# Linear attention and a highway layer: turns of k and q in 64-row tiles, scores and state in equal row halves, gates on Pool, transfers that wait for the fifth last, and a new order

## The chip, the core and the metric

The kernel runs on one core of one Trainium2 chip. The core has a matrix engine (TensorE, PE in the profile; its weight loads are PEld), VectorE (DVE), ScalarE (ACT), GpSimd (POOL) and SyncE (SP, which here only issues transfers), and 16 DMA engines that move data between device memory (DRAM) and the on-chip memory SBUF. TensorE writes its results into PSUM, eight banks of 2 KB per partition, from which DVE or ACT copy them; POOL doesn't read PSUM here. Each engine takes its own instructions in order, and semaphores hold it back where it needs another's result. The metric is device microseconds of the program, as the median of several runs.

## The reference

There are 4 batches, 8 heads, 768 positions and 64 channels. The first part is attention with a decay `lam` per head, in blocks along the sequence with a state of 64 x 64 per head:

```
intra = (qb @ kb^T) * Dmask          # Dmask[i, j] = lam^(i-j) for j <= i
out   = intra @ vb + (qb * lam^(pos+1)) @ kv_state
kv_state = lam^block * kv_state + (kb * lam^(block-1-pos))^T @ vb
```

The second part is a highway layer over the 3072 rows of 512 that come out of it:

```
H = max(x @ w_h, 0);  T = sigmoid(x @ w_t + b_t);  out = T * H + (1 - T) * x
```

All inputs and the output are float32. The inputs q, k and v are 18.9 MB together, the weights 2.1 MB, the output 6.3 MB.

## The kernel before

The work is cut into 12 steps n = 0 to 11, three for each batch, of 256 positions each and all 8 heads. Within a step the positions lie as two halves b of 128. A partition holds two neighbouring positions (j = 0, 1). The powers of `lam` are put into q and v (q times lam^t, v times lam^-t), so that the decay needs no work of its own and the mask is a plain triangle. Heads are taken in pairs hp = 0 to 3, with e = 0, 1 for the head within a pair: channels of head e lie on partitions 64e to 64e+63 of the turned k and q. The highway layer runs on the same steps (here called groups g = 0 to 10; step 11 is cut into the two groups 11 and 12 of 128 rows).

The order is written out by hand: `PLAN` is a list of tokens, and the program emits each token's instructions in that order; each engine then keeps its share of that order. A token such as `TK.3.2=3` is an operation (TK), its step (3), its part (2 means all heads; 0 and 1 are halves), and after `=` the PSUM banks that it uses. `@` names the engine. The tokens:

- `Lk`, `Lq`, `Lv` (L170): one load of 256 KB, half the heads of a step, in pieces of 512 bytes. `W` (L176): one load of 512 KB of the weights. `ST` (L337, L356): a store, 512 KB for a whole step. All of them are issued by SP, in the order of the list. `WC` casts weights to bf16.
- `CK` (L183): k to bf16. `CQ`, `CV` (L190): q and v times their powers, to bf16. Most stand on POOL.
- `TK`, `TQ` (L204): k and q are turned on TensorE against a 128 x 128 identity, 8 matmuls of 128x128 for a whole step. `EK`, `EQ`: the turned values are copied out of PSUM to SBUF, 1024 elements per partition, by ACT or DVE.
- `SS.n.e` (L224): 16 score matmuls of head parity e (on rows 64e to 64e+63 of the array), alternating one by one with the 16 matmuls (L221) that add half b = 1 - e of the step to the state (on the other 64 rows). In the third step of a batch the state after half 1 isn't needed, and `SS.n.0` has scores only. `S` and `U` are the same, apart, for step 0. `KE` copies the state out as the next half's `ss`.
- `M` (L255): a score bank times the triangle, PSUM to SBUF, on DVE. `I` (L271): turned q times the state. `A` (L281): masked scores times v, 16 matmuls of 64x64 tiles for one half of the head pairs. `D`: the result is copied to SBUF as `xT`.
- `F.g.u.w` (L300): 8 matmuls of the highway layer, half u of the output columns, w = 0 for w_h (bank `h`), 1 for w_t (bank `t`). `H` (L305): max(h, 0) - x, on DVE. `G` (L314): the sigmoid on ACT, written back to the PSUM bank. `X` (L318): gate times `hm`, on DVE, giving `th`.
- `R` (L347): x + T (H - x) is turned back to rows, 32 matmuls of 64 rows by 128 columns with 64 moving columns, as two row halves r that write two banks; `E.n.r` (L101 on ACT, L103 on DVE) copies each to the output buffer `o`, of which there are five. The last step is turned by L327 in three parts.
- `Z` (L366): matmuls on a blank tile whose result nobody reads, at the start.

SBUF buffers rotate through pools whose depths stand in `BUFS` (kf, qf and vf, the loaded tiles, have five each). A store or load on SP waits for the semaphore of the transfer eight before it, since eight semaphores are used in turn.

Of the kernel before, what the change touches and what calls it, by code (L numbers as in the profile page):

```python
# [17 lines left out]
Lk.0.0 Lv.0.1 Lv.0.0 Lq.0.0 Lk.0.1 Lq.0.1 Lv.1.1 CK.0.0@POOL Lq.1.0 Z.12=0 TK.0.0=0 Lq.1.1 CV.0.0@DVE Lk.1.0  # L18
CQ.0.0@POOL EK.0.0@DVE Lv.1.0 CV.0.1@DVE CK.0.1@ACT Lk.1.1 Z.11=1 TQ.0.0=1 B=2 EQ.0.0@ACT CQ.0.1@POOL W.0.1 W.0.0
Z.6=0 TQ.0.1=3 TK.0.1=4 EQ.0.1@DVE U.0.0 EK.0.1@ACT W.1.1 S.0.0=56 KE.0.0@DVE S.0.1=01 CQ.1.2@POOL W.1.0 M.0.0.1 Z.1=3  # L20
U.0.1 I.0=34 M.0.1.1 KE.0.1@ACT Lk.2.1 M.0.0.0 A.0.1 M.0.1.0 TQ.1.2=0 Lq.2.1 CV.1.2@DVE CK.1.2@ACT EQ.1.2@ACT Lq.2.0
Z.8=1 TK.1.2=1 A.0.0 EK.1.2@DVE Lk.2.0 D.0.0@DVE Z.3=5 SS.1.1=56 WC.0.0.1@ACT WC.0.0.0@POOL M.1.1.0 KE.1.0@ACT
WC.0.1.0@POOL D.0.1@ACT Lv.2.1 WC.0.1.1@DVE Z.4=0 SS.1.0=01 M.1.1.1 I.1=35 KE.1.1@ACT Lv.2.0 F.0.0.0=4 WC.1.1.0@DVE PT
M.1.0.1 Lk.3.1 F.0.1.0=6 M.1.0.0 WC.1.0.0@POOL WC.1.0.1@ACT Lk.3.0 WC.1.1.1@DVE A.1.1 A.1.0 BC F.0.0.1=1 H.0.1 Lq.3.1
D.1.1@ACT H.0.0 D.1.0@ACT F.0.1.1=0 Lq.3.0 CQ.2.2@POOL F.1.0.0=2 Lv.3.0 G.0.1@ACT CK.2.2@DVE F.1.0.1=6 Lv.3.1
G.0.0@ACT X.0.1@DVE TQ.2.2=5 Lq.4.0 X.0.0@DVE TK.2.2=4 EQ.2.2@ACT CV.2.2@POOL F.1.1.0=3 Lq.4.1 EK.2.2@DVE G.1.0@ACT
H.1.0 SS.2.0=01 Lk.4.1 H.1.1 CK.3.2@POOL SS.2.1=54 Lk.4.0 M.2.0.1 F.1.1.1=2 KE.2.0@ACT M.2.1.0 Lv.4.0 TK.3.2=3 M.2.1.1
CQ.3.2@POOL G.1.1@ACT I.2=15 M.2.0.0 Lv.4.1 A.2.1 X.1.0@DVE A.2.0 Lk.5.0 R.0=40 D.2.0@ACT D.2.1@DVE CV.3.2@POOL
TQ.3.2=6 E.0.0@ACT Lk.5.1 F.2.1.1=1 E.0.1@ACT EQ.3.2@DVE Lq.5.1 EK.3.2@ACT X.1.1@DVE F.2.1.0=5 CQ.4.2@POOL Lq.5.0
R.1=40 H.2.1 SS.3.1=62 Lv.5.0 F.2.0.0=3 CK.4.2@POOL KE.3.0@ACT M.3.1.1 Lv.5.1 E.1.1@ACT M.3.1.0 SS.3.0=52 E.1.0@ACT  # L30
H.2.0 Lq.6.0 TQ.4.2=0 KE.3.1@ACT CV.4.2@POOL M.3.0.1 TK.4.2=6 G.2.1@ACT Lq.6.1 F.2.0.1=4 M.3.0.0 EQ.4.2@ACT EK.4.2@DVE
Lv.6.0 I.3=32 A.3.0 CK.5.2@POOL A.3.1 Lk.6.1 SS.4.1=56 D.3.0@ACT D.3.1@DVE TK.5.2=0 KE.4.0@ACT M.4.1.1 Lk.6.0
F.3.0.0=2 G.2.0@ACT CQ.5.2@POOL EK.5.2@DVE Lv.6.1 SS.4.0=36 H.3.0 F.3.0.1=0 Lq.8.0 M.4.0.0 CV.5.2@POOL M.4.0.1
TQ.5.2=2 Lk.9.0 G.3.0@ACT F.3.1.0=3 X.2.1@DVE Lq.7.0 EQ.5.2@ACT X.2.0@DVE F.3.1.1=6 CQ.6.2@POOL M.4.1.0 Lq.7.1
KE.4.1@ACT I.4=14 H.3.1 G.3.1@ACT R.2=25 Lk.8.1 X.3.0@DVE A.4.0 E.2.1@ACT X.3.1@DVE A.4.1 Lk.7.1 SS.5.0=30 E.2.0@ACT
D.4.0@DVE CK.6.2@POOL SS.5.1=56 D.4.1@ACT Lk.7.0 TQ.6.2=2 M.5.0.0 KE.5.0@ACT CV.6.2@POOL TK.6.2=1 M.5.1.1 Lv.7.0
EQ.6.2@ACT F.4.1.0=4 M.5.0.1 Lv.7.1 EK.6.2@ACT F.4.0.0=3 H.4.1 Lk.8.0 M.5.1.0 I.5=62 SS.6.1=01 H.4.0 Lq.8.1 A.5.0
KE.6.0@ACT M.6.1.0 CQ.7.2@POOL R.3=45 Lv.9.1 A.5.1 M.6.1.1 SS.6.0=30 D.5.0@ACT Lv.8.0 F.4.0.1=1 M.6.0.0 D.5.1@ACT
M.6.0.1 Lk.9.1 TQ.7.2=6 G.4.0@ACT CK.7.2@POOL F.5.0.0=3 Lq.10.1 EQ.7.2@ACT F.4.1.1=2 H.5.0 Lk.10.1 E.3.1@ACT X.4.0@DVE
TK.7.2=0 CV.7.2@POOL G.4.1@ACT I.6=63 ST.0 KE.6.1@DVE F.5.0.1=5 X.4.1@DVE Lv.8.1 F.5.1.0=1 G.5.0@ACT CK.8.2@POOL  # L40
EK.7.2@DVE Lq.9.0 A.6.0 E.3.0@ACT H.5.1 A.6.1 SS.7.1=20 Lq.9.1 D.6.0@ACT D.6.1@DVE TK.8.2=4 M.7.1.1 F.6.1.0=1 Lv.9.0
EK.8.2@ACT X.5.0@DVE CK.9.2@POOL F.6.1.1=6 KE.7.0@DVE Lk.10.0 CQ.8.2@POOL H.6.1 R.4=30 SS.7.0=54 Lk.11.1 E.4.0@ACT
F.5.1.1=1 E.4.1@ACT M.7.0.1 G.6.1@ACT ST.4 M.7.1.0 TK.9.2=3 Lq.10.0 M.7.0.0 TQ.8.2=0 G.5.1@ACT CV.8.2@POOL F.6.0.0=4
EQ.8.2@DVE Lk.11.0 KE.7.1@ACT X.5.1@DVE I.7=25 EK.9.2@ACT Lq.11.0 A.7.0 H.6.0 A.7.1 CQ.9.2@POOL SS.8.0=01 X.6.1@DVE
D.7.1@ACT Lv.10.1 SS.8.1=34 M.8.0.1 D.7.0@ACT F.6.0.1=6 KE.8.0@DVE Lq.11.1 CK.10.2@POOL F.7.0.0=5 M.8.1.0 G.6.0@ACT
M.8.1.1 ST.3 TQ.9.2=1 CV.9.2@POOL H.7.0 F.7.1.0=2 EQ.9.2@ACT Lv.10.0 X.6.0@DVE TK.10.2=3 M.8.0.0 ST.1 I.8=45
EK.10.2@ACT CQ.10.2@POOL H.7.1 SS.9.1=61 A.8.1 KE.9.0@ACT M.9.1.0 A.8.0 R.5=02 M.9.1.1 SS.9.0=36 CK.11.2@POOL
E.5.1@DVE F.7.0.1=1 KE.9.1@ACT M.9.0.1 E.5.0@ACT F.7.1.1=2 D.8.0@DVE D.8.1@ACT ST.5 CQ.11.2@POOL M.9.0.0 G.7.0@ACT
Lv.11.1 TK.11.2=6 Lv.11.0 I.9=04 F.8.1.0=5 EK.11.2@ACT ST.2 X.7.0@DVE TQ.10.2=3 G.7.1@ACT H.8.1 CV.10.2@POOL F.8.0.0=1
EQ.10.2@ACT R.6=65 H.8.0 A.9.1 X.7.1@DVE A.9.0 SS.10.1=31 D.9.0@ACT D.9.1@DVE F.8.1.1=2 E.6.1@ACT M.10.1.1 F.9.1.0=0  # L50
E.6.0@DVE G.8.1@ACT M.10.1.0 ST.6 TQ.11.2=4 CV.11.2@POOL KE.10.0@DVE F.9.1.1=5 EQ.11.2@ACT X.8.1@DVE SS.10.0=16
G.9.1@ACT H.9.1 R.7=32 M.10.0.1 KE.10.1@ACT F.8.0.1=4 X.9.1@DVE E.7.0@ACT M.10.0.0 E.7.1@ACT I.10=06 SS.11.0=53
G.8.0@ACT ST.7 A.10.0 M.11.0.0 A.10.1 SS.11.1=21 D.10.1@ACT X.8.0@DVE F.9.0.0=5 KE.11.0@ACT M.11.1.0 D.10.0@ACT
F.9.0.1=6 M.11.0.1 M.11.1.1 F.10.1.0=4 G.9.0@ACT H.9.0 I.11=20 X.9.0@DVE A.11.0 A.11.1 R.8=31 D.11.0@ACT R.9=56
E.8.0@ACT F.10.0.0=2 E.9.0@DVE E.9.1@ACT E.8.1@ACT D.11.1@DVE ST.9 F.10.1.1=3 H.10.0 ST.8 F.10.0.1=6 H.10.1 G.10.1@ACT
F.12.1.1=5 G.10.0@ACT X.10.1@DVE F.11.1.1=1 F.11.1.0=0 G.12.1@ACT X.10.0@DVE F.11.0.1=2 G.11.1@ACT H.11.1 F.12.1.0=4
R.10=36 G.11.0@ACT H.12.1 X.11.1@DVE F.11.0.0=0 E.10.0@ACT X.12.1@DVE F.12.0.1=4 E.10.1@ACT H.11.0 F.12.0.0=1
G.12.0@ACT X.11.0@DVE ST.10 R.11.1.1=5 H.12.0 R.11.0.2=3 E.11.1.1@DVE X.12.0@DVE E.11.0.2@ACT ST.11.1.1 R.11.1.0=0
ST.11.0.2 E.11.1.0@DVE ST.11.1.0
"""  # L60

BUFS = dict(kf=5, qf=5, vf=5, kb=3, qb=2, vs=3, kT=2, qT=2, m=8, xT4=2, th4=2, xT2=3, xT1=2, th2=2, th1=2, hm2=3, hm1=2, tb2=2, tb1=2, ss=4, o=5, oh=2, oq=1)
# [3 lines left out]
def kernel(  # L66
# [11 lines left out]
    nc = tc.nc  # L78
# [67 lines left out]

    def groups(n, b):
        return ((n,), b) if n < N - 1 else ((n, b), 0)

    def new(key, shape, dtype=BF16, tag=None):  # L150
        if key not in made:
            tag = tag or key[0]
            made[key] = sb.tile(shape, dtype, tag=tag, name=tag, bufs=BUFS[tag])
        return made[key]

    def bank(key, i, shape, dtype=F32):
        if key not in made:
            made[key] = ps.tile(shape, dtype, tag=f"b{i}", name=f"b{key[0]}", bufs=1)
        return made[key]
# [8 lines left out]
    SRC = {"k": k, "q": q, "v": v}  # L168

    def load(x, n, p, eng):  # L170
        b, c = divmod(n, NST)
        hs = heads(p)
        (A if eng else nc.sync).dma_start(out=new((x + "f", n), [128, H, J * D], F32)[:, hs],  # L173
                          in_=SRC[x][b, hs, c * 2 * C:(c + 1) * 2 * C, :].rearrange("h (p j) d -> p h (j d)", j=J))

    def load_w(w, g):  # L176
        nc.sync.dma_start(out=w_f[w][:, 2 * g:2 * g + 2],
                          in_=(moe_w_h, moe_w_t)[w][256 * g:256 * g + 256].rearrange("(kc p) m -> p kc m", p=128))

    def cast_w(w, g, i, eng):  # L180
        copy(eng, w_b[w][:, 2 * g + i], w_f[w][:, 2 * g + i])
# [17 lines left out]
    def trans(x, n, p, bk):  # L199
        hs = heads(p)  # L200
        t = bank((x + "tr", n, p), bk[0], [128, (hs.stop - hs.start) // 2, J, C], BF16)
        for i, h in enumerate(range(hs.start, hs.stop, 2)):
            for j in range(J):
                T.transpose(t[:, i, j, :], get(x + "b", n)[:, j, h:h + 2, :], id128)  # L204

    def evac_k(n, p, eng):
        hs = heads(p)
        copy(eng, new(("kT", n), [128, NP, J, C])[:, hs.start // 2:hs.stop // 2], get("ktr", n, p))

    def evac_q(n, p, eng):  # L210
        hs = heads(p)
        copy(eng, new(("qT", n), [128, NP, J, C])[:, hs.start // 2:hs.stop // 2], get("qtr", n, p))


    def score(n, e, hp, j, b):
        T.matmul(get("s", n, e, hp // 2)[half(b), hp % 2, j, :], lhsT=get("kT", n)[half(e), hp, j, half(b)],  # L216
                 rhs=get("qT", n)[half(e), hp, :, half(b)], start=True, stop=True)
# [6 lines left out]
    def scores_state(n, e, bk):  # L224
        for u in range(2):
            bank(("s", n, e, u), bk[u], [128, 2, J, C])
        b = 1 - e
        st = [(hp, j, x) for hp in range(NP) for j in range(J) for x in range(2)]
        if b == 1 and n % NST == NST - 1:
            st = []  # L230
# [188 lines left out]
```

## Time and profile before

Four runs took 108.48, 108.48, 108.53 and 109.37 us, median 108.51. The profiled execution is the one of 109.37 us; its span, from the first to the last instruction, is 107.3 us, and 2.07 us lie around it.

| engine | busy us | share of the span |
|---|---|---|
| TensorE matmuls | 99.4 | 93% |
| TensorE weight loads | 80.6 | 75% |
| DVE | 82.4 | 77% |
| ACT | 71.8 | 67% |
| POOL | 55.6 | 52% |

From HBM 20.98 MB are read and 6.29 MB written. Matmuls are pipelined: a single one is shown with 0.19 to 0.27 us, but they start much closer together, so a group's cost on TensorE is read from the start of one group to the start of the next, or from the chain that ended last, which shows these differences. The same holds for DVE, where instructions of 512 elements last 0.68 us and start 0.60 us apart when nothing holds them. In the page's slices each digit is the busy share of one fortieth of the span (2.7 us) in tenths.

### The profile page before, as it was taken

The page shows a single profiled execution, that of the slowest core. Times are in us where ns is not written, and L with a number is a line of the kernel's source. Part 1 is how long each engine was busy: PE and PEld are TensorE (multiplying, and loading weights), DVE is VectorE, ACT ScalarE, POOL GpSimd, SP SyncE. Part 2 cuts the span into 40 slices and gives each one's busy share as a digit, 9 for nine tenths or more (in the row PEclk, how much of TensorE's full clock was granted, in tenths as well). Part 3 has the DMA queues.
Part 4 walks back from the last instruction along what each step waited for, and adds up shares of the span by engine and source line. Part 5 has one row for each costly group of instructions (what it writes and reads, how often), then busy time and mean ns, then how long its engine had stood idle before and what let it go on. Part 6 is the DMA issues. An engine that isn't in the chain of part 4 may idle for free.

```text
span 107.3 us, 4970 instructions
## 1 busy us (share of the span) xinstructions
PE 99.4 (93%) x2190; PEld 80.6 (75%) x2190; DVE 82.4 (77%) x140; ACT 71.8 (67%) x129; POOL 55.6 (52%) x46
## 2 busy tenths in 40 slices
PE   4986999999999989999999999999999999999950
PEld 1332665488987869899989888989897888889930
DVE  1233495879799786999995996999976998958860
ACT  3303244686875668689859785987696798687940
POOL 7028340427978976997548593999691700000000
PEclk9999999999999999999999999999999999999999
DMA  0899999999999999999999999999979254108264
GB/s 3 229 303 287 293 354 383 326 291 274 294 284 270 292 288 273 299 288 275 296 302 296 301 347 283 322 281 304 365 275 305 104 194 173 37 6 321 76 245 145
DMA packets 42701, 27.59 MB, mean 257 GB/s; under 512 B 1588, under 2 KB 38712, under 8 KB 42680
## 3 DMA queue, kind: packets, MB, share of 16 engines
q1 hardware_dynamic: 42528, 27.27, 86.6%
q8 instruction: 17, 0.28, 1.1%
q14 instruction: 4, 0.03, 0.1%
q10 hardware_dynamic: 152, 0.01, 0.1%
HBM read 20.98 MB, written 6.29 MB: 254 GB/s over the span
## 4 chain that ended last, share of the span: by engine, by line
PE 78%; DVE 6%; DMA 5%; issue 2%; POOL 1%; SPq 1%; ACT 1%; POOLq 0%; DVEq 0%
PE bt L300 19%; PE bh L300 18%; PE bs L216 8%; PE bo L281 6%; PE bx L347 6%; PE bqtr L204 6%; DMA qf<-in_q_dram 5%; PE bktr L204 5%; PE bspin L366 5%; PE bo L271 4%; DVE m L255 4%; PE kv L221 2%; POOL qb L190 1%; DVE hm L305 1%; SPq L173 1%
## 5 line engine op out<-in xcount | busy, mean ns | idle before, releaser
L300 PEld LDWEIGHTS <-w_b 128*128 128x128 bf16 x416 | 36.4, 98 | 4.9 <-issue 0.4
L255 DVE TENSOR_TENSOR m<-bs,tri 128x512 bf16<-128x512 f32 x48 | 31.0, 680 | 2.3 <-PE bs L216 2.1
L190 POOL TENSOR_TENSOR qb<-qf,pow_q 128x1024 bf16<-128x1024 f32 (+1 forms) x13 | 23.6, 1812 | 9.4 <-DMA qf<-in_q_dram 8.4
L314 ACT ACTIVATE bt<-bt,bt_col 128x256 f32<-128x256 f32 (+1 forms) x52 | 22.0, 432 | 5.5 <-PE bt L300 2.9
L300 PE MATMUL bh<-xT,w_b 128*128 128x256 bf16 (+1 forms) x208 | 25.0, 265 | 0.2 <-issue 0.2
L300 PE MATMUL bt<-xT,w_b 128*128 128x256 bf16 (+1 forms) x208 | 24.5, 265 | 0.0
L190 POOL TENSOR_TENSOR vs<-vf,pow_v 128x1024 bf16<-128x1024 f32 x10 | 19.0, 1904 | 7.0 <-DMA vf<-in_v_dram 6.0
L305 DVE SCALAR_TENSOR_TENSOR hm<-bh,xT 128x512 bf16<-128x512 f32 (+1 forms) x26 | 16.5, 643 | 4.0 <-PE bh L300 2.5
L318 DVE TENSOR_TENSOR th<-bt,hm 128x512 bf16<-128x512 f32 (+1 forms) x26 | 16.5, 642 | 2.0 <-ACT bt L314 1.9
L101 ACT ACTIVATE xT<-bo 128x512 bf16<-128x512 f32 x16 | 11.6, 749 | 4.6 <-PE bo L281 4.6
L216 PE MATMUL bs<-qT,kT 64*64 64x128 bf16 x384 | 13.9, 218 | 0.6 <-issue 0.3
L366 PE MATMUL bspin<-blank,id 128*128 128x512 bf16 x45 | 12.6, 425 | 1.4 <-POOL id masks.py:199 1.4
L103 POOL CAST kb<-kf 128x1024 bf16<-128x1024 f32 (+1 forms) x10 | 10.0, 995 | 6.9 <-DMA kf<-in_k_dram 5.8
L101 ACT ACTIVATE ss<-kv 128x512 bf16<-128x512 f32 x15 | 8.9, 596 | 6.4 <-PE bs L216 5.2
L216 PEld LDWEIGHTS <-kT 64*64 64x64 bf16 x384 | 10.9, 106 | 2.6 <-issue 1.1
L101 ACT ACTIVATE o<-bx 128x512 f32<-128x512 f32 x19 | 10.4, 595 | 1.4 <-PE bx L347 1.3
L101 ACT ACTIVATE qT<-bqtr 128x1024 bf16<-128x1024 bf16 (+1 forms) x10 | 9.8, 980 | 1.8 <-PE bqtr L204 1.8
L281 PE MATMUL bo<-m,vs 64*64 64x128 bf16 x384 | 9.1, 219 | 0.4 <-DVE m L255 0.4
L366 PEld LDWEIGHTS <-id 128*128 128x128 bf16 x45 | 4.4, 107 | 6.7 <-issue 2.2
L221 PE MATMUL kv<-vs,kb 64*64 64x64 bf16 x320 | 9.2, 196 | 0.0
L204 PE MATMUL bqtr<-id,qb 128*128 128x128 bf16 x96 | 7.5, 220 | 0.9 <-POOL qb L190 0.9
L101 ACT ACTIVATE kT<-bktr 128x1024 bf16<-128x1024 bf16 (+1 forms) x7 | 6.8, 970 | 1.9 <-PE bktr L204 1.9
(50 smaller groups left out, 108.7 us busy)
## 6 DMA issues: line engine op xcount, KB each, us to landing
kf<-in_k_dram SPq DMA_DIRECT2D x24, 256.0 KB, 5.3
vf<-in_v_dram SPq DMA_DIRECT2D x24, 256.0 KB, 5.5
qf<-in_q_dram SPq DMA_DIRECT2D x24, 256.0 KB, 5.6
out_dram<-o SPq DMA_DIRECT2D x11, 512.0 KB, 4.8
w_f<-in_moe_w_h_dram SPq DMA_DIRECT2D x2, 512.0 KB, 6.6
w_f<-in_moe_w_t_dram SPq DMA_DIRECT2D x2, 512.0 KB, 8.6
out_dram<-oh SPq DMA_DIRECT2D x2, 128.0 KB, 2.0
out_dram<-oq SPq DMA_DIRECT2D x1, 256.0 KB
```

The costliest lines, as they stand in the source:

```text
L101: A.activation(dst, src, AF.Copy)
L190: ENG[eng].tensor_tensor(dst, in0=get(src, n)[:, heads(p)].rearrange("p h (j d) -> p h j d", j=J), in1=pw[:, n % NST, heads(p), :, None].t ...
L204: T.transpose(t[:, i, j, :], get(x + "b", n)[:, j, h:h + 2, :], id128)
L216: T.matmul(get("s", n, e, hp // 2)[half(b), hp % 2, j, :], lhsT=get("kT", n)[half(e), hp, j, half(b)], rhs=get("qT", n)[half(e), hp, :, ha ...
L221: T.matmul(kv[half(e), hp, half(e)], lhsT=get("kb", n)[half(b), j, 2 * hp + e, :], rhs=get("vs", n)[half(b), 2 * hp + e, j, :], start=firs ...
L255: V.tensor_tensor(new(("m", n, e, u), [128, 2, J, C]), in0=get("s", n, e, u), in1=tri[:, None].to_broadcast([128, 2, J, C]), op=ALU.mult)
L281: T.matmul(get("o", n, b)[half(e), hp, :], lhsT=get("vs", n)[half(b), 2 * hp + e, j, :], rhs=get("m", n, e, u)[half(b), hp % 2, j, :], sta ...
L300: T.matmul(t[:, r, :], lhsT=w_b[w][:, kc, (2 * u + r) * 128:(2 * u + r + 1) * 128], rhs=get("xT", *g)[:, kc, :], start=(kc == 0), stop=(kc ...
L305: V.scalar_tensor_tensor(new(("hm", g, u), [128, 2, z * C], tag=f"hm{z}"), in0=get("h", g, u), scalar=0.0, in1=get("xT", *g)[:, 2 * u:2 * ...
L314: A.activation(dst[:, r, :], src[:, r, :], AF.Sigmoid, bias=bt_col[:, 2 * u + r:2 * u + r + 1])
L318: ENG[eng].tensor_tensor(new(("th", g), [128, NP, z * C], tag=f"th{z}")[:, 2 * u:2 * u + 2, :], in0=get("tt", g, u), in1=get("hm", g, u), ...
L366: T.matmul(t, lhsT=id128, rhs=blank, start=True, stop=True)
```

## The change

Five things are changed at once.

1. *Turns.* For steps 2 to 11, `T.n` takes the place of `TK` and `TQ`: 32 transpositions in tiles of 64 rows by 128 columns against a 64 x 64 identity, the two row halves r alternating and writing two banks, each with k and q together. `ET.n.r` copies one bank into a tile `kq` that holds both; still two copies of 1024 elements for a step.
2. *Scores and state.* `SA.n` and `SB.n` take the place of the two `SS`. The matmuls are put on two rows of work, one for each 64-row half, and merged by their summed weights (56 for a score pair, 32 for a state pair). `SA`: the state pairs of half 0 and four score pairs on the lower rows, eight score pairs of head parity 1 on the upper. `SB`: the other four score pairs on the lower rows, the state pairs of half 1 on the upper.
3. *Gates.* For nine gates (g, u) = (2, 1) to (10, 1) the sigmoid is written to an SBUF tile `tb`, and the multiplication runs on POOL.
4. *Transfers.* From the seventeenth on, each transfer on SP waits for the fifth last to have landed. Weights are loaded by halves of their columns, in pieces of 1 KB instead of 2 KB.
5. *Order and buffers.* The list is a new one, and each tile names its SBUF buffer. `I` is now per half of a step. There are 24 spins (14, 8, 2) instead of 45. q and k of step 0 and q of step 1 are loaded first, the weights after step 2. Of the stores, two (steps 1 and 4) stand ahead of the last load instead of five. Of the copies of T, 12 are on DVE and 8 on ACT (before, of whole-step EK and EQ, 7 on DVE and 15 on ACT). Of the copies E of whole steps, 8 instead of 3 are on DVE, of the copies D 11 instead of 8.

```diff
+AHEAD = 5
+FILL = 16
+POOL_GATES = [(2, 1), (3, 1), (4, 1), (5, 1), (6, 1), (7, 1), (8, 1), (9, 1), (10, 1)]
...
+    def send(dma):
+        dma = dma.ins if hasattr(dma, "ins") else dma
+        if len(sent) >= FILL:
+            tc.add_manual_dep(dma, sent[-AHEAD], WAIT, reason="transfers under way")
+        sent.append(dma.name)
...
+    def trans_both(n):
+        for r in range(2):
+            bank(("tr", n, r), [128, 2, NP, J, 64], BF16)
+        for i, x in enumerate("kq"):
+            for hp in range(NP):
+                for j in range(J):
+                    for r in range(2):
+                        T.transpose(get("tr", n, r)[:, i, hp, j, :], get(x + "b", n)[half(r), j, 2 * hp:2 * hp + 2, :], id128[half(r), half(r)])
+
+    def evac_both(n, r, eng):
+        copy(eng, kq(n)[:, :, :, :, half(r)], get("tr", n, r))
...
-    def scores_state(n, e, bk):
...
-        for i, (hp, j, x) in enumerate((hp, j, x) for hp in range(NP) for j in range(J) for x in range(2)):
-            score(n, e, hp, j, x)
-            if st:
-                state(n, b, *st[i])
+    def tiles(*rows):
+        todo = sorted((sum(w for w, _ in row[:i]), r, i) for r, row in enumerate(rows) for i in range(len(row)))
+        for _, r, i in todo:
+            for go in rows[r][i][1]:
+                go()
+    def scores_state_a(n):
...
+        tiles(state_pairs(n, 0) + score_pairs(n, 0, (0, 1)), score_pairs(n, 1, range(NP)))
+    def scores_state_b(n):
...
+        tiles(score_pairs(n, 0, (2, 3)), [] if n % NST == NST - 1 else state_pairs(n, 1))
...
+        made["tt", g, u] = new(("tb", g, u), [128, len(rows(g, u)), size(g) * C], F32) if (g, u) in POOL_GATES else t
```

The end of the new order, from the second store on:

```
ST.4 I.9.1=2 A.9.0=1 A.9.1 D.9.0@DVE=0 CK.10.2@POOL=1 E.5.1@ACT X.6.1@POOL G.7.0 X.7.0@DVE=0 D.9.1@ACT T.10=54
ET.10.1@DVE=1 Lv.10.1=0 Lk.11.0=1 R.6=60 E.6.0@ACT=4 I.8.1=1 F.9.0.1=2 I.8.0=3 F.9.1.0=6 E.6.1@DVE A.8.0 A.8.1
Lv.10.0 CV.10.2@POOL=1 Lq.11.0 CQ.11.2@POOL=2 ET.10.0@DVE G.9.0 SA.10=405 H.9.1=0 D.8.0@ACT=2 Lv.11.0=1 D.8.1@DVE
X.7.1@POOL F.9.0.0=6 M.10.1.0=1 I.10.0=1 M.10.1.1=6 F.8.1.1=3 F.8.1.0=0 Lv.11.1 KE.10.0@ACT=3 I.10.1=5 M.10.0.0=5
A.10.0 H.9.0=1 X.9.0@DVE=1 SB.10=4 Lk.11.1 ST.2 CK.11.2@POOL=2 T.11=62 G.8.1=1 ET.11.0@ACT=0 H.8.1=2 R.7=30
E.7.0@ACT=2 E.7.1@ACT M.10.0.1=7 A.10.1 D.10.0@DVE=1 KE.10.1@DVE=2 ST.3 F.9.1.1=4 F.8.0.0=6 H.8.0=1 F.8.0.1=3
D.10.1@DVE CV.11.2@POOL=3 ET.11.1@ACT SB.11=1 G.9.1=0 SA.11=026 M.11.1.0=3 M.11.1.1=4 M.11.0.1=0 M.11.0.0=2
...
```

## The prediction

> **What bounds the kernel now.** I read the page's busy shares and slices first, then the window from 31.6 to 100 us, then the chain that ended last, and last the queues of POOL and SP.
>
> ```profile
> PE 99.4 (93%) x2190; PEld 80.6 (75%) x2190; DVE 82.4 (77%) x140; ACT 71.8 (67%) x129; POOL 55.6 (52%) x46
> ...
> PE   4986999999999989999999999999999999999950
> ...
> POOL 7028340427978976997548593999691700000000
> PEclk9999999999999999999999999999999999999999
> DMA  0899999999999999999999999999979254108264
> GB/s 3 229 303 287 293 354 383 326 291 274 294 284 270 292 288 273 299 288 275 296 302 296 301 347 283 322 281 304 365 275 305 104 194 173 37 6 321 76 245 145
> ```
>
> TensorE is full from slice 9 on, and the DMA engines are full until slice 30 (about 83 us), at about 290 GB/s where only q, k and v move. So two resources are near their ends, the transfers some 20 us earlier than TensorE. In the window TensorE rests 0.7 of 68.4 us:
>
> ```profile
> 31.60:100.00 68.40, 67.72 (x1709) 59.60 (x1708) 59.77 (x98) 52.62 (x96) 40.97 (x26) 1.00 0.87 260
> ```
>
> Columns: length, then busy PE, weight loads, DVE, ACT, POOL, granted clock, DMA share, GB/s. TensorE's work sets the end; a microsecond taken from it there is gained, as long as data comes in time. The chain (start, length, what) prices the tokens:
>
> ```profile
> 47.38 0.87 PE bt L300 x8
> 48.26 0.45 PE bo L271 x8
> 48.70 0.57 PE bx L347 x32
> 49.27 0.57 PE bo L281 x32
> ...
> 55.95 0.98 PE bt L300 x8
> 56.93 0.45 PE bqtr L204 x8
> ```
>
> An F block is 0.87, a whole transposition (TK or TQ) 0.45, an R of 32 matmuls in 64-row tiles 0.57. The block at 55.95, behind 64x64 tiles, takes 0.98: a change of tile shape costs 0.10. Without it R is 0.48, an A (half of the 0.57 behind R) 0.24, an I 0.22 for each half.
>
> **TensorE, removed and added.** (a) For steps 2 to 11, T replaces TK and TQ. Its 32 matmuls have the shape of R's (64 rows by 128 columns, 64 moving), which is 0.48. Per step 0.45 + 0.45 - 0.48 = 0.42; ten steps 4.2 us. (b) Scores and states:
>
> ```profile
> 65.41 0.24 PE L216 MATMUL bs<-qT,kT 64*64 64x128 bf16 x1
> ...
> 65.98 1.05 PE L300 MATMUL bt<-xT,w_b 128*128 128x256 bf16 x8
> ```
> ```profile
> 13.62 0.44 PE L221 MATMUL kv<-vs,kb 64*64 64x64 bf16 x16
> 13.99 0.40 PE L271 MATMUL bo<-qT,ss 128*128 128x128 bf16 x4
> ```
>
> An SS lasts 65.98 - 65.41 = 0.57, 0.47 without the change of shape: eight score pairs, 59 ns each, beside shorter states. Sixteen states alone last 13.99 - 13.62 - 0.10 = 0.27, 34 ns a pair. SA then needs 8 x 34 + 4 x 59 = 0.51 on one half and 0.47 on the other; SB 0.27, or 0.24 in the four steps without late states. Twelve steps: 12 x 0.51 + 8 x 0.27 + 4 x 0.24 = 9.2 instead of 24 x 0.47 = 11.3, 2.1 saved. (c) Counting along the two orders, the shape changes 59 times before and 77 times after: 18 x 0.095 = 1.7 lost. Net 4.6 us less. The spins fall from 45 to 24 at 0.215, 4.5 us, but stand where TensorE waits for the first data, so I count nothing. TensorE alone would end 4.6 us earlier: span 102.7.
>
> **Clock.** The first eight spins start 0.43 us apart, until 4.8 us, the rest 0.215; after that no wait reaches 1.5 us. With fewer spins, the gap between the first fourteen (done near 6.1) and the first transposition (q lands near 5.5, one Pool multiply) is 1 to 2 us. [...]
>
> **Transfers.** As built, every load already waits for the transfer eight before it, whose semaphore it reuses; five replaces eight from the seventeenth on. Only other transfers stand behind on SP. Loads are issued every (57.71 - 24.84) / 36 = 0.91 us:
>
> ```profile
> 24.84 1.29 SPq L173 DMA_DIRECT2D qf<-in_q_dram  x2
> ...
> 57.71 0.51 SPq L173 DMA_DIRECT2D qf<-in_q_dram  x1
> ```
>
> The first lands at 5.5 (below). 512 KB at 321 to 365 GB/s is 1.6 us for a store; weights took about 1.5, and with pieces of 1 KB instead of 2 KB I take 1.6 (bounds 1.5, and 1.8 at the loads' rate). Test on before: the last load follows 71 others, four weights and five stores: 5.5 + 71 x 0.91 + 6 + 8 = 84.1; POOL's wait for it ended at 83.8. In the new order only two stores stand ahead of the last load, which lands at 5.5 + 71 x 0.91 + 6 x 1.6 = 79.7, 4 us earlier. The deferred stores fit: the ninth whole store could be down by 93. One is close: on ACT, E.7 reuses the output buffer that ST.2 frees at 81.3, and behind it on ACT stands the second copy of T.11, which SB.11 needs; R.7, which E.7 needs anyway, ends near 83, so it costs nothing unless the loads are late.
>
> **POOL.**
>
> ```profile
> 5.52 0.61 POOL L103 CAST kb<-kf 128x512 bf16<-128x512 f32 x1 [2.84 <-DMA kf<-in_k_dram]
> 8.24 1.57 POOL L190 TENSOR_TENSOR qb<-qf,pow_q 128x512 bf16<-128x512 f32 x1 [2.11 <-DMA qf<-in_q_dram]
> 9.97 1.04 POOL L190 TENSOR_TENSOR qb<-qf,pow_q 128x512 bf16<-128x512 f32 x1 [0.16 <-DMA qf<-in_q_dram]
> ...
> 83.79 1.91 POOL L190 TENSOR_TENSOR vs<-vf,pow_v 128x1024 bf16<-128x1024 f32 x1 [3.02 <-DMA vf<-in_v_dram]
> ```
>
> Nine gates of 512 elements move here at 1.04 each (1.57 for the one beside a DVE multiply of two SBUF inputs, which the new order has only at the start). They cost more than the 0.68 on DVE, but DVE gives up 9 x 0.60 (its pitch) while it takes on five more copies of turns, five of `o`, three of `xT` and two fewer of the state, 11 x 0.60: about even. In each step's 5.5 us of transfers POOL now holds 1.9 + 1.9 + 1.0 + 1.0 = 5.8: nearly full, and a casting of v behind a gate waits for it. [...] The row of the same size decides for 1.04.
>
> **Where TensorE can't run ahead.** Work left counts blocks along the new order. From SA.10: ten F (8.7), eight half F (3.6), four I halves (0.9), four A (1.0), SA and SB twice (1.5), T (0.5), four R (1.9), three last turns (0.9), twelve changes of shape (1.1): 20.1 us. SA.10 needs v of step 10: 67 loads after the first and six larger ones, 5.5 + 61.0 + 9.6 = 76.1, then 1.9 on POOL: 78.0. So TensorE can't end before 98.1. The same count gives 96.9 from T.3 (k lands 31.0, cast 32.1, 64.8 left), 97.8 from SA.6 and 97.9 from SA.8; T.11, through POOL, 97.6. Data, POOL and TensorE become bounds together, so 1.2 us of the 4.6 is given back, and waits on each other are added: 0.8 us (what before lost behind its own R.7: 16.2 of work from 87.1, last matmul 103.9) and as much, my estimate, at the joints. Last matmul 99.8; before needs 3.5 us from there (copy, store, landing). **Span 103.3** against 107.3. The profiled run took 109.4, 2.07 more than its span, and stands 0.86 above the median of 108.5; on the median's scale 103.3 + 2.07 - 0.86 = **104.5 us**.
>
> Evacuations of T are as many as before, 1024 elements each; the new target has runs of 64. I price them like the 0.69 on DVE and 1.03 on ACT; if DVE falls to its rate of one f32 element (1.2), twelve cost 6 us on an engine with about 8 spare, and that goes to rival B.
>
> **Rivals.** A, data come sooner or joints cost nothing: 101.5 to 102.8. For it: the clean rows of DMA; against: before's pace was steady. B, the coupled engines give most of it back: POOL with gates of 1.57 (+3 us on k of step 11), or slow evacuations; 106.4 to 109.6, take 107.5. For it: four resources above 85% at once; against: POOL's rows hardly vary (1.902 to 1.907). C, slower: five transfers under way don't fill the engines. Place: SP, from the seventeenth transfer. A load lands a median 5.3 to 5.6 us after its issue now, of which an unknown part is queueing; the lone 128 KB stores at the end land in 2.0. If 5.5 us were all latency, five in flight give 1.1 us a load; 52 loads before SA.10 x 0.19 = 10 us, and the time is 114. It decides from a pace of 1.0 (latency and transfer above 5.0 us): 52 x 0.09 = 4.7 eats the gain. Against: 2.0 plus 0.9 is under 3. D, five frees nothing either: the wait does nothing, which is in the forecast.
>
> **Chances.** Forecast 0.58 (102.8 to 106.4), A 0.12, B 0.20 (0.08 of it under 107.4), C 0.10. A measurement tells about 1% from no change, so 107.4 to 109.6 is the same: faster 0.78, same 0.12, slower 0.10. The range 102.3 to 108.8 leaves out a third of A and all of C.
>
> **What would show it.** T at 0.48 to 0.57 per 32; SA near 0.51, SB near 0.27; T.11 near 82 us; last load landed near 80; POOL 60 us or more busy with gates near 1.04; TensorE's idle time behind POOL. Wrong if loads are spaced 1.0 or more, if gates or copies of T are far longer, or if TensorE idles behind banks not yet copied out.

## The result, and the profile after

The changed kernel takes 111.37 us (median of 12 runs, 109.58 to 116.48), the kernel before 108.79 (17 runs beside them, 108.48 to 110.33). The ratio is 1.0123, 95% interval 1.0083 to 1.0163: slower by over 1%, where 104.5 us was forecast. The ratio leaves out runs that lie more than 1.5% above the fastest of their kernel (in the changed one seven, from 111.35 us on), which is why it is smaller than that of the medians. The profiled execution took 110.32 us, its span is 108.3.

The page after, busy times and slices:

```profile
PE 95.0 (88%) x2329; PEld 76.0 (70%) x2329; DVE 83.5 (77%) x142; ACT 63.3 (58%) x119; POOL 68.7 (63%) x59
...
PE   4998379959999998996999999995959999999950
...
POOL 6035797597298968986796999699399400804000
PEclk9999965699999999999999999999999999999996
DMA  0799999999999999999999999999997502802684
GB/s 5 216 305 290 290 290 294 300 320 343 293 269 303 290 292 282 278 266 292 280 283 289 279 283 291 306 357 304 254 381 269 218 0 81 312 6 78 244 315 143
```

TensorE has less work, but its row is no longer full: a 6, a 5 and again a 5 stand among the nines. POOL has 13 us more, the DMA engines are full as before, and the clock has a dip in slices 6 to 8. The window from 31.6 to 100 us (length, then busy PE, weight loads, DVE, ACT, POOL, clock, DMA share, GB/s):

```profile
31.60:100.00 68.40, 64.41 (x1799) 54.34 (x1798) 59.54 (x96) 44.49 (x83) 49.19 (x34) 1.00 0.84 251
```

TensorE rests 4.0 us there, 0.7 before. What it waits for between 30 and 100 us (the view of waits: us in total, times, longest):

```profile
PE kv L260 <- issue: 1.5, 2, 1.2
PE btr L248 <- issue: 1.1, 1, 1.1
PE bx L393 <- issue: 1.1, 1, 1.1
PE bo L323 <- DVE m L297: 0.2, 1, 0.2
```

"issue" is time in which the engine waited for nothing that the profile shows: no data, bank or other engine. 3.7 of its 3.9 us of waits here are of this kind. The chain that ended last shows where (start, length, what):

```profile
49.84 0.72 PE btr L248 x30
50.56 1.15 issue
51.71 0.21 PE btr L248 x2
...
74.27 0.04 PE kv L260 x3
74.34 1.23 issue
75.56 0.22 PE kv L260 x2
...
79.13 0.44 PE bx L393 x30
79.56 1.11 issue
80.68 0.20 PE bx L393 x2
```

Each stands in the middle of a burst: T.6 stops before its last two transpositions, SB.9 amid its states, R.6 before its last two matmuls.

**What these places have in common.** I numbered TensorE's matmuls and weight loads in the trace. All three stops, and a short one of 0.30 us at 42.0, lie at an index of 192 above a multiple of 256. The page also lists a DMA queue of kind "instruction" with 18 packets of 16 KB (17 in the kernel before), one ahead of each such block of 256:

```profile
q8 instruction: 18, 0.29, 1.2%
```

From the trace of the changed kernel (us; the delay counts from the first instruction of the block before):

```
block   starts   fetch issued, delay   packet took   packet's end to start   stop before it
1472    42.34          2.07               1.15              1.41                 0.30
1984    51.72          1.77               1.16              1.52                 1.15
3264    75.56          2.67               0.89              1.61                 1.23
3520    80.68          2.78               1.01              1.32                 1.11
4032    90.14         -0.79               1.16              2.64                 none
```

Here no block starts sooner than 1.28 us behind the end of its packet, the least lead. While loads run (33 to 82 us) the delay has a median of 1.87 us and the packet takes 1.06: with the 1.28, 4.2 us for a block, and more where the delay is longer (2.78 makes it 5.1). Without their stops the blocks before the four late ones would have taken 3.3 to 4.3 us, less than their successors needed to arrive. With their stops the blocks took 4.75 us in the mean, against 5.20 before. Behind 86 us, where few loads are left, the delay is -0.8 to 0.6.

**Where the time went.** For each moment, the moment plus the array time still to do (the prediction's prices: F 0.87, T and R 0.48, TK 0.45, SA 0.51 and so on) is the time at which TensorE could end at best. It rises wherever TensorE loses time:

```
at us              24     36     44     52     68     76     84     100
before            102.0  102.5  103.1  102.8  102.9  102.8  103.1  103.0
after              98.0   98.1   98.7  100.3  100.9  102.3  103.6  103.9
e2_turns_128      101.5  101.6  101.7  102.0  102.8  103.7  103.6  103.7
e7_no_loads        98.1  100.5  100.7  100.9  101.5  101.9  102.0  102.2
```

At 36 us the changed kernel still has its whole gain, 4.4 us, and stands at 98.1, the number that the prediction computed from SA.10. Then it loses 5.8 us where before loses 0.5; the steps to 52, 76 and 84 hold the stops shown above. The four stops are 3.8 us. The other 2.0 are not stops: the kernel with the turns taken back (third row) loses as much with 0.5 us of stops.

### The profile page after: what moved, and what is told of

Its sections match the earlier page's. It is cut to its first block, busy times and chain, and to the rows that moved or that the text cites. A ratio compares the mean times of both kernels' runs of the same rounds, so it can differ in the third digit from the quotient of the medians.

```text
span 108.3 us, 5265 instructions
## 1 busy us (share of the span) xinstructions
PE 95.0 (88%) x2329; PEld 76.0 (70%) x2329; DVE 83.5 (77%) x142; ACT 63.3 (58%) x119; POOL 68.7 (63%) x59
## 4 chain that ended last, share of the span: by engine, by line
PE 64%; DMA 10%; SPq 9%; DVE 6%; issue 5%; POOL 2%; ACT 1%; DVEq 0%; POOLq 0%
PE bh L349 19%; PE bt L349 18%; SPq L200 9%; PE bo L323 5%; PE bx L393 5%; DMA qf<-in_q_dram 5%; PE btr L248 5%; DMA vf<-in_v_dram 5%; PE bs L255 5%; PE bo L312 3%; PE kv L260 3%; DVE m L297 2%; DVE th L363 2%; POOL vs L218 2%; DVE hm L353 1%
## 5 line engine op out<-in xcount | busy, mean ns | idle before, releaser
L349 PEld LDWEIGHTS <-w_b 128*128 128x128 bf16 x416 | 36.3, 98 | 4.9
L218 POOL TENSOR_TENSOR vs<-vf,pow_v 128x1024 bf16<-128x1024 f32 (+1 forms) x13 | 22.1, 1705 | 8.7 <-DMA vf<-in_v_dram 5.7
L360 ACT ACTIVATE bt<-bt,bt_col 128x256 f32<-128x256 f32 (+1 forms) x34 | 14.2, 422 | 6.6 <-PE bt L349 5.6
L363 POOL TENSOR_TENSOR th<-tb,hm 128x512 bf16<-128x512 f32 x9 | 10.4, 1158 | 10.1 <-ACT tb L360 7.0
L255 PE MATMUL bs<-kq 64*64 64x128 bf16 x384 | 13.4, 228 | 0.0
L363 DVE TENSOR_TENSOR th<-bt,hm 128x512 bf16<-128x512 f32 (+1 forms) x17 | 10.5, 623 | 1.1 <-ACT bt L360 0.3
L260 PEld LDWEIGHTS <-kb 64*64 64x64 bf16 x320 | 7.7, 115 | 5.0 <-issue 4.3
L122 ACT ACTIVATE kq<-btr 128x1024 bf16<-128x1024 bf16 x8 | 8.2, 1022 | 4.9 <-PE btr L248 4.9
L255 PEld LDWEIGHTS <-kq 64*64 64x64 bf16 x384 | 9.7, 112 | 1.2 <-issue 1.0
L411 PE MATMUL bspin<-blank,id 128*128 128x512 bf16 x24 | 8.6, 525 | 1.4 <-POOL id masks.py:199 1.4
L360 ACT ACTIVATE tb<-bt,bt_col 128x256 f32<-128x256 f32 x18 | 7.6, 478 | 3.8 <-PE bt L349 3.8
```

Of the source, the lines that this page charges most:

```text
L122: A.activation(dst, src, AF.Copy)
L218: ENG[eng].tensor_tensor(dst, in0=get(src, n)[:, heads(p)].rearrange("p h (j d) -> p h j d", j=J), in1=pw[:, n % NST, heads(p), :, None].t ...
L260: T.matmul(kv[half(e), hp, half(e)], lhsT=get("kb", n)[half(b), j, 2 * hp + e, :], rhs=get("vs", n)[half(b), 2 * hp + e, j, :], start=firs ...
L349: T.matmul(t[:, r, :], lhsT=w_b[w][:, kc, m * 128:(m + 1) * 128], rhs=xT(g)[:, kc, :], start=(kc == 0), stop=(kc == KC - 1))
L360: A.activation(get("tt", g, u)[:, r, :], t[:, r, :], AF.Sigmoid, bias=bt_col[:, m:m + 1])
L363: ENG[eng].tensor_tensor(new(("th", g), [128, NP, size(g) * C], tag=f"th{size(g)}")[:, span(g, u), :], in0=get("tt", g, u), in1=get("hm", ...
```

## The experiments

Theory S (instruction supply) is as above. Its rivals: theory C (fewer spins, so the clock is halved), POOL and the gates (rival B), and the number of transfers under way (rival C of the prediction). Stops are given as the "issue" waits of TensorE between 30 and 100 us, 3.7 us in the changed kernel, 0.5 in the kernel before.

### More spins, and fewer in the kernel before

```diff
- ... SA.0=613 ... TK.1.0=1 ... A.0.1=3 ... T.2=24 ... SA.2=542
+ ... Z.6=6 SA.0=613 ... Z.4=1 TK.1.0=1 ... Z.3=3 A.0.1=3 ... Z.4=2 T.2=24 ... Z.3=5 SA.2=542
```

> Twenty spins more (44 in all, before has 45), between 11 and 24 us of the span, where TensorE of the changed kernel waits for data; nothing else differs. Theory C (the clock: 24 spins leave TensorE so little work from 10 to 23 us that its clock is halved for two or more stretches of 3.4 us): the granted clock is 1.00 in every slice from 8 us to the tail in every run, runs agree within 0.5% and the median falls from 111.4 to 108.5 to 109.5 us. Theory S (instruction supply: TensorE stands still about 1.2 us where a block of 256 of its instructions is not there in time; some 4.4 us in the profiled run): these stalls stay, but at other tokens, since 40 more instructions lie ahead of them: still at indices of 192 above a multiple of 256, so that the stall in T.6 leaves T.6. If neither holds the time is 111.4 and the stalls stand in the same tokens.

110.51 us (109.89 to 111.47), ratio 1.0134 (1.0082 to 1.0186); clock 0.989 to 1.000 in every run, stops 3.4 us. The chain now stops elsewhere:

```profile
59.13 1.42 issue
60.55 0.38 PE bt L349 x2
...
75.12 1.27 issue
76.39 0.32 PE bx L393 x10
...
80.46 0.62 issue
81.08 0.49 PE bx L393 x22
```

T.6 is free of it; an F block and two R have it, at indices 2496, 3264 and 3520, again 192 above multiples of 256. So the stops belong to the index, not to a token, and no bank or engine is behind them. The clock was repaired and the ratio stayed, so theory C is not the cause of the loss: TensorE starts the block of index 960 (spins counted) at 33.57 us, in the changed kernel at 33.17, so the full clock brought it nothing up to there. None of the six runs took 112 us or more, and the median is 0.9 us lower.

```diff
- Z.11=1 ... Z.6=0 ... Z.1=3 ... Z.8=1 ... Z.3=5 ... Z.4=0      (kernel before)
+ Z.10=1 ... Z.2=3
```

> The kernel before with 24 spins instead of 45 (the early 12, 10 and 2 stay; the 6, 8, 3 and 4 behind them go). Theory C: the clock falls to 0.5 for stretches between 10 and 25 us, as in the changed kernel, the times spread over several per cent and the median is 1 to 3 us above 108.5. If the spins are needless, as the prediction had it: 108.5, clock 1.00 throughout.

109.43 us (107.95 to 111.33, 12 runs), ratio 0.9992 (0.9947 to 1.0036), clock 0.948 to 0.984. The clock falls as theory C says and the runs spread, but the ratio shows no cost, and the fastest run has a mean clock of 0.960. In the profiled one (108.70 us) the clock is halved from 11.6 to 15.0 us, and the block of index 960, with 42 spin instructions fewer ahead of it, starts at 34.17; before at 34.10.

### The turns taken back

```diff
- T.3=46 ... ET.3.1@DVE=0 ... ET.3.0@ACT
+ TK.3.2=4 TQ.3.2=6 ... EQ.3.2@DVE=0 ... EK.3.2@ACT      (so for steps 2 to 11)
```

> The ten T of the changed kernel are taken back to whole transpositions, 8 of k and 8 of q of 128 x 128, into the same two banks; 320 fewer TensorE instructions, 4.2 us more array time by the prediction's rows; all other orders as after. If array time on TensorE sets the end (the prediction's sum): 111.4 + 3 to 4 = about 115. Theory S: fewer and longer instructions let the supply keep up, so stalls of over 1 us become fewer and the time stays within 1 us of the changed kernel's 111.4, or below it. Theory P (copies of T or POOL are late): the copies lose their runs of 64 and the time falls by more than 1 us with the idle time behind ACT and DVE.

111.14 us, ratio 1.0183 (1.0129 to 1.0236), as good as the changed kernel; stops 0.5 us. 4.2 us of array time came back and 3.2 us of stops went. The windows from 36 to 80 us, of the changed kernel and of this one, say the same:

```profile
36.00:80.00 44.00, 40.69 (x1216) 33.70 (x1208) 38.98 (x64) 30.17 (x56) 36.58 (x25) 1.00 1.01 292
```
```profile
36.00:80.00 44.00, 43.19 (x1109) 36.28 (x1102) 38.59 (x62) 30.65 (x56) 35.30 (x24) 1.00 0.98 278
```

TensorE rests 3.3 us in the first, 0.8 in the second, and both are equally fast. So the supply explains why the turns gained nothing, but not the whole loss. Without T the prediction's sum leaves 2.1 - 1.7 = 0.4 us of gain, and this kernel is 1.8% slower than the one before. In the profiled runs its last matmul ends 1.0 us later than before, and 0.7 us more lie behind it; where in the new order they are lost was not traced.

### Twice the cost: more instructions, the same array time

```diff
+            for c in ([slice(0, 128), slice(128, 256)] if 4 <= g <= 7 else [slice(0, size(g) * C)]):
-                         rhs=xT(g)[:, kc, :], ...
+                             rhs=xT(g)[:, kc, c], ...
```

> The changed kernel with the sixteen F blocks of steps 4 to 7 written as twice as many matmuls over half as many columns: 256 more instructions of TensorE (128 matmuls, 128 weight loads), between some 38 and 75 us, with about the same array time (eight of 128 columns take 0.44 to 0.45, so a split block 0.88 to 0.90 instead of 0.87: 0.5 us in all at most). If array time or data set the end: 111.4 + 0 to 0.5. Theory S (a block of 256 instructions needs 4.75 us under load, the mean from 33 to 81 us in the changed kernel): one block more, + 3 to 4.8 us, 114.4 to 116, and TensorE stands still at more block boundaries.

118.0 us (116.12 to 120.91), ratio 1.0679 (1.0554 to 1.0805) where the changed kernel has 1.0123: 6.6 us more by the medians, about 6 by the ratios. The array accounts for 0.3 (a split block free of stops takes 0.89 instead of 0.87). Stops 7.1 us:

```profile
PE btr L248 <- issue: 3.6, 2, 2.1
PE bt L350 <- issue: 1.4, 1, 1.4
PE bh L350 <- issue: 1.2, 1, 1.2
```

The whole is not the price of the 256 instructions. In the profiled run (118.19 us, not the shortest; the changed kernel's 110.32) the block of index 960, which lies ahead of the first split block, starts 2.8 us later (35.95 instead of 33.17). From there to the start of the last block 5.0 us are lost: 3.4 by more stops, 0.3 by array time, and 1.3 that fit a clock halved from 56.1 to 59.5 us (last section). So theory S had the direction and, with 3 to 4.8 us, about the size of this part; the time of 118 holds more.

> The same split in the kernel before. Its blocks of 256 take 4.5 to 5.9 us between 34 and 81 us, 5.2 in the mean, so it has some 0.4 us to spare in each of nine. Theory S: of the 4.75 us of one block more about 3.5 are covered, + 0.5 to 2.5 us, 109.5 to 111.5, with stalls that before lacks. Array time alone: 109 to 109.5.

111.32 to 114.31 us in four runs, median 113.88, beside 109.2 of the kernel before. Only the run of 111.32 held a clock of 1.000: 2.1 us more, as theory S had it, but a single run. In the profiled one (114.31) the clock is halved from 80.0 to 83.4 us. Its stops are 3.3 us, where the kernel before had 0.5:

```profile
PE bh L301 <- issue: 1.8, 1, 1.8
PE bo L281 <- issue: 1.5, 1, 1.5
```

256 instructions with hardly any array time make both kernels slower, and of the theories only S expected that. The new one seems to lose more; with a single run of the old one at full clock this is not shown.

### Without the loads

```diff
+        if n > 1:
+            slots.clear()
+            made[x + "f", n] = made[x + "f", n % 2]
+            return
```

> The changed kernel with the loads of q, k and v left out from step 2 on: the castings of later steps read what the loads of steps 0 and 1 left (same work on every engine, other values). Weights and stores are still moved. Theory S with fetches delayed by data: a fetch starts within 0.6 us of the first instruction of the block before, as it does in the changed kernel behind 86 us, no stall of over 0.5 us is left between 30 and 100 us, TensorE's work is done as soon as its count allows (the bound of 98.1 us of the prediction, less what the start gains), and the time is 100 to 105 us. Theory S without that (a block takes its 4 to 5 us whatever the data does): the stalls stay, 108 us or more. If the loads themselves were the bound: the time falls with no stall to begin with.

106.78 us (103.96 to 108.6): 103.96 in the run with a clock of 0.992, within the 100 to 105 expected, and more in the three others with 0.952 to 0.984. In the profiled one (108.6) the clock is halved from 17.8 to 28.1 us; from the block of index 960 to the last block it is still 4.1 us faster than the changed kernel (63.4 instead of 67.4). Stops 0.3 us; the fetches' delay has a median of 0.68 instead of 1.87 us. The same window, with a DMA share of 15%:

```profile
36.00:80.00 44.00, 43.55 (x1276) 36.39 (x1268) 41.35 (x67) 33.14 (x61) 32.88 (x23) 1.00 0.15 52
```

The same instructions flow almost without stops once the DMA engines are nearly free. TensorE of the changed kernel had no wait for data behind 30 us, so what left with the loads was the delay of the fetches.

### The wait for the fifth last

```diff
-FILL = 16
+FILL = 999          (e5)
-AHEAD = 5
+AHEAD = 3           (e6; e8 with the twenty spins)
```

> The changed kernel without the wait for the fifth last transfer; the wait for the eighth last, by the reused semaphore, stays. Rival C (the wait starves the DMA engines): the last load lands 2 us or more before 81 us and the time falls by 1 us or more. Theory S, with the fetches of TensorE's instructions queueing behind data: more data under way, so a fetch starts later behind the first instruction of the block before it (1.6 to 2.8 us in the changed kernel under load) by 0.5 to 2 us, more stalls, 112 to 115 us. If the number under way matters to neither: 111.4, within 0.5%.

> The changed kernel with the wait for the third last transfer instead of the fifth last. Theory S with queueing: fetches start 0.5 to 1.5 us sooner behind the block before, the stalls of over 1 us go, 107 to 109 us, if three under way still move a load per 0.9 us. Rival C: loads come every 1.1 us or more, the last lands behind 90 us, 115 us or more. If the number under way matters to neither: 111.4.

> The two edits of the twenty early spins and of the wait for the third last together. If theories S (with queueing) and C both hold: 106 to 108 us, below the kernel before, with the clock at 1.00 in each run. If the third last starves the loads: as the run with the third last alone.

Without the wait 114.91 us, ratio 1.0547 (1.0467 to 1.0627). A load lands 5.5 us after its issue instead of 4.8, and the last one at 82.6 instead of 81.1. Stops rise to 4.6 us, but the fetches' delay only from 1.87 to 2.09, less than theory S expected, and most of the loss lies ahead of the stops: the block of index 960 starts 3.0 us later (36.2 instead of 33.2), the last block 4.5. TensorE's wait for weights is 1.1 us of these 3.0.

With the third last 125.12 us, ratio 1.147 (1.1349 to 1.159), with spins 127.94. The delay does fall, to 1.35 us, and one stop of 1.3 is left, but loads are starved, and with the third last alone the chain is one of transfers:

```profile
DMA 65%; PE 10%; SPq 10%; POOL 5%; issue 3%; DVE 3%; ACT 0%; DVEq 0%; POOLq 0%
```

From transfer 40 to 77, counted from zero, a load takes 49.1 / 39 = 1.26 us, at the fifth last 36.3 / 39 = 0.93 (two of the 37 are stores of twice the size). So what rival C describes does happen, at three under way and not at five.

> The kernel before with the wait for the fifth last transfer from the seventeenth on, and nothing else of the change. In the changed kernel's order this wait was worth 3.5 us against none. Theory S, with fetches of instructions delayed by data under way: before has few stalls to lose, so at most 0.5 us less, 108.3 to 109. If the wait helps by which piece lands first (fewer under way, so the next one needed is not behind later ones): 1 us less or more, 107 to 108. If before's order, which issues loads as buffers come free and mixes stores in, is starved by it: 111 or more.

110.46 us (108.62 to 112.65, 12 runs) beside 109.36, ratio 1.0027 (0.998 to 1.0075): the wait alone gains nothing in the old order. The fetches' delay falls from 2.09 to 1.16 us, but there were hardly any stops to lose. What the wait is worth in the new order lies mostly ahead of 36 us; of that only the 1.1 us at the weights are explained.

### The gates, and mixtures

```diff
- X.2.1@POOL
+ X.2.1@DVE           (so for all nine)
```

> The nine gates on POOL go to DVE, in the same place of the order; the sigmoid still leaves its result in SBUF. POOL loses 9 x 1.16 = 10.4 us of work, DVE gains about 9 x 0.62 = 5.6. If POOL's nearness to its limit delays the castings (prediction's rival B): the castings from step 4 on come 1 to 3 us sooner and the time falls by 1 to 3 us. If DVE is the tighter of the two: slower by 1 to 3 us. Theory S and theory C: within 1 us of the changed kernel, with the same stalls of TensorE.

120.66 us (115.3 to 122.61). Even the run of 115.3, which is the profiled one, is more than the 1 to 3 us slower that were expected if DVE is the tighter. POOL falls to 59.7 us, and TensorE's turns wait for gates that now stand in DVE's line:

```profile
PE bx L393 <- DVE th L363: 5.2, 4, 1.8
```

The gates are right on POOL in this order. Nor was POOL's nearness to its limit the loss: of TensorE's 3.9 us of waits in the changed kernel none is behind POOL.

```diff
- T.4=46 ... T.6=35 ... T.9=20 ... T.10=54
+ TK.4.2=4 TQ.4.2=6 ... TK.6.2=3 TQ.6.2=5 ... TK.9.2=2 TQ.9.2=0 ... TK.10.2=5 TQ.10.2=4
```

> The changed kernel with whole transpositions in steps 4, 6, 9 and 10 alone (128 instructions fewer, 4 x 0.42 = 1.7 us more array time). Theory S: 128 instructions at 4.75 us per 256 are 2.4 us of supply; the end is the later of the two, so 1 to 2 us less than the changed kernel, 109.5 to 110.5. Array time: 113.

> The same four steps, with the twenty early spins, which gave 0.9 us less than the changed kernel with a clock of 0.99 to 1.00. If the two add: 108.5 to 109.5, about the time of the kernel before. If the spins cost array time where instructions set the pace: as the run with the four steps alone.

> The changed kernel with whole transpositions in steps 4, 6, 9 and 10 and the twenty spins (109.9 us), and the wait for the sixth last transfer in place of the fifth last. Between the fifth last (109.9) and none (3.5 us more in the changed kernel): 110.5 to 111.5 if each further transfer under way costs about 1.2 us; 109.9 if the fifth and the sixth are alike; below 109 if five starve some load.

Four turns taken back: 110.85 us (12 runs), ratio 1.0076 (1.0025 to 1.0127), stops 2.1 us. With spins: 109.91 (12 runs), 1.0087 (1.0044 to 1.013), stops 0.6. With the sixth last besides: 111.52, 1.0126 (1.0057 to 1.0195), stops 3.4. The mixtures trade stops for array time at nearly even rates; none beats the kernel before, which stood at 109.2 and 109.4 beside them.

## Why the prediction was wrong

**The step that failed** is the sum under "TensorE, removed and added": "Net 4.6 us less. [...] TensorE alone would end 4.6 us earlier". It priced array time and took TensorE's time for it. The ten T add 320 instructions to TensorE's stream (the 42 fewer of the spins lie at the start), in its densest bursts, and while the loads ran a block of 256 needed some 4.2 us to arrive (median delay, packet and least lead). By that, one and a quarter blocks more are an estimated 5.3 us of supply for 4.2 us of array time saved. The runs showed 3.8 us of stops at the starts of blocks; with the T taken back 0.5 were left and the time was the same. The profile before held the hint: 17 instruction packets, a block per 5.2 us with packets ending 1.6 to 2.5 us ahead of use, and a first short stop at the start of a block:

```profile
39.26 0.31 issue
```

The order of instructions was counted, but their number was not priced. The same sum also failed in a smaller part whose cause stays open: without T it leaves a gain of 0.4 us, and the run without T lost 1.8%.

**Most sizes were right.** With their change of shape (0.10) T takes 0.57, as R does, and SA 0.58 in the median, as priced; SB takes 0.35 to 0.48 (0.37 priced). At 24 us the possible end had fallen from 102.0 to 98.0, and at 36 us it was 98.1, as computed from SA.10. SA.10 then came at 83.6 instead of 78.0 and T.11 at 87.9 instead of near 82, behind a full line of work with the stops in it; TensorE waited for neither v nor k. The last matmul ends at 105.0 instead of 99.8: 3.8 of these 5.2 us are stops, the rest was not traced. The term of 0.8 us for the joints doesn't follow from the numbers beside it (87.1 + 16.2 against 103.9 is 0.6), which moves the forecast by less than 0.5 us.

**Clock.** The prediction's sum holds nothing for the clock. The clock did fall. Windows of the changed kernel, with the busy PE behind the length and the clock third from the end:

```profile
7.40:10.80 3.40, 3.11 (x30) 1.81 (x28) 1.15 (x3) 1.56 (x2) 1.58 (x1) 1.00 1.21 291
10.80:14.20 3.40, 1.62 (x52) 1.24 (x51) 2.85 (x6) 1.58 (x3) 2.46 (x3) 1.00 1.20 290
14.20:17.60 3.40, 2.81 (x65) 2.06 (x66) 3.40 (x8) 0.16 (x1) 2.78 (x4) 0.50 1.20 293
```

With spins in the second of these windows it is busy for 2.87 us and the clock stays:

```profile
10.80:14.20 3.40, 2.87 (x72) 1.64 (x73) 2.85 (x6) 1.26 (x3) 2.79 (x3) 1.00 1.21 290
```

So here a window half busy came ahead of a fall, with no wait longer than 1.8 us in it. That the sum holds nothing for it did no harm, by luck: the fall cost nothing that the ratio shows in the kernel before with 24 spins, and the full clock gained nothing in the changed kernel with spins.

**Transfers.** The last load landed at 81.1 instead of 79.7, and stores fitted. "D, five frees nothing either" was wrong in this order: without the wait it is 3.5 us slower by the medians. Rival C fell at five.

**POOL and copies.** 68.7 us busy, as announced (60 or more). The prediction called 5.8 us of work in 5.5 "nearly full"; between 36 and 80 us POOL is busy for 36.6 of 44.0. The nine gates took 1.16 each, not 1.04, and the copies of T what was priced:

```profile
L363 POOL TENSOR_TENSOR th<-tb,hm 128x512 bf16<-128x512 f32 x9 | 10.4, 1158 | 10.1 <-ACT tb L360 7.0 <-ACT xT L122 3.0
...
L122 ACT ACTIVATE kq<-btr 128x1024 bf16<-128x1024 bf16 x8 | 8.2, 1022 | 4.9 <-PE btr L248 4.9
L124 DVE COPY kq<-btr 128x1024 bf16<-128x1024 bf16 x12 | 8.1, 682 | 1.6 <-PE btr L248 1.6
```

TensorE hardly idles behind POOL. Rival B expected most of the gain to be given back, but by coupled engines; none of the rivals named the supply of instructions, and the time lies above the range.

## What to carry to other kernels

Where TensorE is nearly full, price instructions beside array time: count its matmuls and weight loads, and compare the time in which TensorE works off 256 of them with the time in which the trace shows a block arriving (here 4.2 us at the median delay under full load, up to 5.1). An edit that halves the array time of a step with twice the instructions gains only as far as that allows. "issue" in the middle of a burst, always at the same index modulo 256 (192 in the changed kernel and with more spins), was the sign of it here.

## What the hardware showed beyond that

The fetch of instructions pays for the loads beside it: its delay is 1.87 us with them and 0.68 without. That it queues behind them on the DMA engines fits, but the trace doesn't show the queue. Where TensorE stopped at the start of a block, that cost 0.3 to 1.2 us in the changed kernel and up to 2.1 us with split blocks.

The clock was halved right behind a window of 3.40 us in which TensorE was busy for 1.62 us. In this trace it stayed so for 6.8 us, from 14.2 to 21.0; the other falls named above lasted 3.4 us (11.6 to 15.0, 56.1 to 59.5, 80.0 to 83.4) and 10.3 (17.8 to 28.1). No threshold follows from it: in the kernel before with split blocks TensorE was busy for 1.63 of the 3.40 us from 56.1, and the clock stayed at 1.00 in the next 3.4 us.

A fall can follow a stop too. Two windows of the changed kernel with split blocks, the first with a stop of 2.07 us at 53.3:

```profile
52.00:55.40 3.40, 1.33 (x73) 1.03 (x63) 1.89 (x3) 1.16 (x3) 2.47 (x2) 1.00 0.99 279
55.40:58.80 3.40, 3.40 (x78) 3.15 (x81) 2.17 (x4) 1.92 (x3) 2.78 (x2) 0.60 0.83 237
```

In the second the mean clock is 0.60, and an F block in it takes 1.52 us instead of 0.89: there the late block cost twice. In the changed kernel's own profiled run no stop did that; its clock is 1.00 from 21.1 to 106.4 us. What makes its runs of 112 to 116 us (mean clock 0.928 to 0.985) stays open: neither the six runs with more spins, which have the stops, nor the six with the turns taken back, whose mean clocks (0.955 to 0.983) are as low as in many of the changed kernel's, hold one.
